# Three score chunks on each side of A@V: regrouping the bursts of a fused attention and feed-forward kernel

## The chip, the cores and the metric

The kernel runs on one core of a Trainium2 chip. The metric is the device time of one execution in microseconds (us); the time before is the median of five executions.

## The reference

For each of 8 batches and 12 heads, attention without a softmax over 448 positions of 64 features; then a feed-forward layer with a parametric ReLU over the 3584 x 768 result.

```python
scores = scale * np.matmul(q, k.transpose(0, 1, 3, 2))      # scale = 1/8
attn = np.maximum(scores, 0.0) ** 2 / S                     # S = 448
attn_out = np.matmul(attn, v)
x = attn_out.transpose(0, 2, 1, 3).reshape(B * S, H * D)    # 3584 x 768
h = x @ w_in                                                # 768 x 2048
g = np.maximum(h, 0.0) + alpha * np.minimum(h, 0.0)
out = g @ w_out                                             # 2048 x 768
```

## The kernel before, in words

**Units of work.** Four heads of one batch form a group; there are 24 groups, three to a batch. A group is cut into seven score *chunks*. `score_mm` (L171) does a chunk with four matmuls of 64x64 weights over 448 columns, which occupy the four quarters of the TensorE array together, so four of them take the place of one ("a wave"). A chunk fills two neighbouring PSUM banks. `relu` (L182) takes both banks to SBUF in one instruction, on ScalarE (line 185) for a chunk marked "A", on VectorE (line 187) for one marked "D". `square` (L190) squares it in SBUF, on VectorE (L195) or ScalarE (L193). `attnv` (L198) multiplies the seven squared chunks of a group by V: 28 matmuls in seven waves (L205) into a pair of banks, whose first bank ScalarE (L215) and whose second bank VectorE (L216) then scale into `xT`.

`f1` (L252) makes one of 16 blocks of the hidden layer of a batch: six 128x128 matmuls over 448 columns (L239), then ScalarE (L247) and VectorE (L248) evict it into `gT`. `f2` (L257) makes 128 rows by 384 columns of the output: 16 matmuls (L262), one copy out of PSUM (L264, on ScalarE), and two output DMAs from SyncE's queue (L270).

**PSUM.** There are eight banks, handed out in the program's order. `take_bank` gives the bank that was taken longest ago; `take_pair` gives the pair (0-1, 2-3, 4-5, 6-7) whose later-taken bank was taken longest ago:

```python
lo = min((0, 2, 4, 6), key=lambda i: (max(taken[i], taken[i + 1]), i))
i = min(range(8), key=lambda i: (taken[i], i))
```

The first matmul into a bank waits until the engine that evicts the bank's last content is done.

**Order.** It is written out by hand; every engine runs its instructions in the order of the program. `sc` (L220) does chunks up to the relu, `sq` (L225) the squares that are still due, `run` (L230) both. A *plain burst* is `run(some(3))`: three chunks between two `f1` or two `f2`. A *full burst* is `burst(n)` (L394): three chunks, `attnv(n)`, two chunks, all squares on VectorE. Chunks marked A, D, A in turn (`some`, L389).

Groups 0 to 5 and the first hidden layer are an opening written out line by line up to L383. From L386 on, chunks of groups 6 to 23 are taken from one list. During batch 1 (L401 to L438) there are four plain bursts and full bursts 6, 7 and 8. Then the loop over batches 2 to 7 (L440): 16 `f1`, with plain bursts ahead of blocks 6 and 12, then six or eight `f2` units with three full bursts, each behind an `f2`. The last batch has no bursts. In batch 6 the list runs out: its second full burst has only one chunk behind `attnv`, its third none.

**Loads.** `prepare(n)` (L343) readies group n: two copies on VectorE (L162), a DMA transpose into `T` from SyncE's queue (L164), and the loads of q, k and v of group n+2 from GpSimd's queue (L97, L104). `turn_pe` (L143) does the same with 28 transposes on TensorE and two copies.

Of the kernel before, what the change touches and what calls it, by code (L numbers as in the profile page):

```python
# [16 lines left out]
NJ = 7  # L17
# [3 lines left out]
def kernel(  # L21
# [10 lines left out]
    nc = tc.nc  # L32
    B, H, S, D = q.shape
# [6 lines left out]
    HALF = d_model // 2  # L40
# [43 lines left out]
    def take_bank():  # L84
        i = min(range(8), key=lambda i: (taken[i], i))
        take(i, 1)
        return psum[:, i]
# [4 lines left out]
    def load_qk(n):  # L92
        b, g = divmod(n, NG)
        for name, src in (("q", q), ("k", k)):
            t = raw_pool.tile([128, 2, NJ, D], BF16, tag=name, name=f"{name}raw")
            flat = src[b].rearrange("(m two) (pp j) d -> (two pp) m (j d)", two=2, j=NJ)
            nc.gpsimd.dma_start(out=t.rearrange("p m j d -> p m (j d)"), in_=flat[:, 2 * g:2 * g + 2])  # L97
            raw[(n, name)] = t
# [44 lines left out]
    def turn_pe(n, cuts=((0, NJ, "D"),), cuts_k=((0, NJ, "D"),)):  # L143
        t = T_pool.tile([128, 2, NJ, 128], BF16, tag="T", name="T")
        for i, name in enumerate("qk"):
            src = raw.pop((n, name))
            for lo, hi, eng in (cuts, cuts_k)[i]:
                ps = take_bank().bitcast(BF16)
                for j in range(lo, hi):
                    for s in range(2):  # L150
                        nc.tensor.transpose(ps[64 * s:64 * s + 64, 128 * j:128 * j + 128], src[:, s, j], ident)  # L151
                dst = t[:, i, lo:hi].rearrange("p j c -> p (j c)")
                if eng == "D":
                    nc.vector.tensor_copy(dst, ps[:, 128 * lo:128 * hi])  # L154
                else:
                    nc.scalar.copy(dst, ps[:, 128 * lo:128 * hi])
        T[n] = t

    def turn_dma(n):
        p = perm_pool.tile([128, 2, NJ, 2, D], BF16, tag="perm", name="perm")  # L160
        for i, name in enumerate("qk"):
            nc.vector.tensor_copy(p[:, i], raw.pop((n, name)).rearrange("p s j d -> p j s d"))  # L162
        t = T_pool.tile([128, 2, NJ, 128], BF16, tag="T", name="T")
        nc.sync.dma_start_transpose(out=t.rearrange("p a j c -> p (a j) c"),  # L164
                                    in_=p.rearrange("p a j s d -> p (a j s d)"))
        T[n] = t
# [4 lines left out]
    def score_mm(n, j):  # L171
        ps = take_pair()
        t = T[n]
        for r in range(2):
            for c in range(2):
                nc.tensor.matmul(ps[64 * c:64 * c + 64, r, :S],  # L176
                                 t[64 * r:64 * r + 64, 1, j, 64 * c:64 * c + 64],
                                 t[64 * r:64 * r + 64, 0, :, 64 * c:64 * c + 64],
                                 start=True, stop=True)
        return ps  # L180

    def relu(ps, eng):  # L182
        rl = rl_pool.tile([128, 2, S], BF16, tag="rl", name="rl")
        if eng == "A":
            nc.scalar.activation(rl, ps[:, :, :S], ACTF.Relu)  # L185
        else:
            nc.vector.tensor_scalar(rl, ps[:, :, :S], 0.0, None, ALU.max)  # L187
        return rl

    def square(n, j, rl, eng="D"):  # L190
        a = at_pool.tile([128, 2, S], BF16, tag="at", name="at")
        if eng == "A":
            nc.scalar.activation(a, rl, ACTF.Square)  # L193
        else:
            nc.vector.tensor_tensor(a, rl, rl, ALU.mult)  # L195
        att[(n, j)] = a

    def attnv(n):  # L198
        ps = take_pair()
        vv = vraw.pop(n)  # L200
        for j in range(NJ):
            a = att.pop((n, j))
            for r in range(2):
                for s in range(2):
                    nc.tensor.matmul(ps[64 * s:64 * s + 64, r, :S],  # L205
                                     vv[64 * r:64 * r + 64, s, j, :],
                                     a[64 * r:64 * r + 64, s],
                                     start=(j == 0), stop=(j == NJ - 1))
        b, g = divmod(n, NG)
        if g == 0:  # L210
            xT[b] = xT_pool.tile([128, NG, 2, S], BF16, tag="xT", name="xT")
        if n == 0:
            nc.scalar.activation(xT[b][:, g], ps[:, :, :S], ACTF.Copy, scale=out_scale)
            return
        nc.scalar.activation(xT[b][:, g, 0], ps[:, 0, :S], ACTF.Copy, scale=out_scale)  # L215
        nc.vector.tensor_scalar(xT[b][:, g, 1], ps[:, 1, :S], out_scale, None, ALU.mult)  # L216
# [3 lines left out]
    def sc(chunks):  # L220

        for n, j, eng in chunks:
            late.append((n, j, relu(score_mm(n, j), eng)))

    def sq(k=99, eng="D"):  # L225
        for g in late[:k]:
            square(*g, eng)
        del late[:k]

    def run(chunks):  # L230
        sc(chunks)
        sq()
# [21 lines left out]
        f1_mm(ps, b, ff, range(KM))  # L254
        f1_out(ps, b, ff)

    def f2(sb, c, hf, parts=((0, HALF),)):  # L257
        o = o_pool.tile([128, HALF], F32, tag="o", name="osb")
        for lo, hi in parts:
            ps = take_bank()[:, :hi - lo]  # L260
            for ff in range(KF):
                nc.tensor.matmul(ps, gT[sb][:, ff, bass.ts(c, 128)], w_out_sb[:, hf, ff, lo:hi],  # L262
                                 start=(ff == 0), stop=(ff == KF - 1))
            nc.scalar.copy(o[:, lo:hi], ps)  # L264
            for u in range(2):
                blk = 2 * c + u
                b, j = 2 * sb + blk // NJ, blk % NJ
                rows = out[b * S:(b + 1) * S].rearrange("(pp j) d -> j pp d", j=NJ)
                eng = nc.scalar if u and hi - lo < HALF else nc.sync
                eng.dma_start(out=rows[j][:, hf * HALF + lo:hf * HALF + hi], in_=o[64 * u:64 * u + 64, lo:hi])  # L270


    pat = "ADAAAAA"
# [1 line left out]
    def ch(n, lo, hi, p=pat):  # L275
        return [(n, j, p[j]) for j in range(lo, hi)]
# [57 lines left out]
    def f1s(b, lo, hi):  # L334
        for ff in range(lo, hi):
            f1(b, ff)

    def load(n):
        if n < NQ:
            load_qk(n)  # L340
            load_v(n)

    def prepare(n):  # L343
        if n < NQ:
            turn_dma(n)
        load(n + 2)
# [9 lines left out]
    ps = take_bank()[:, :S]  # L356
# [5 lines left out]
    f1s(0, 10, 12)  # L362
    sc(ch(3, 6, 7) + ch(4, 0, 2, "AA"))
    f1s(0, 12, 16)
    f2(0, 0, 0)
    sc(ch(4, 2, 5, "AAADAAA"))
    attnv(3)
    sc(ch(4, 5, 7, "AAAAAAD"))
    turn_pe(5)
    sq(3)  # L370
    sq(2, "A")
    load_qk(8)
    load_v(8)
    f2(0, 1, 0)
    sc(ch(5, 0, 3))
    attnv(4)
    sc(ch(5, 3, 5, "AAAADAA"))
    sq(3)
    sq(2, "A")
    f2(0, 2, 0)  # L380
    sc(ch(5, 5, 7, "AAAAAAD"))
    sq(1, "A")
    sq(1)  # L383


    chunks = [(n, j) for n in range(2 * NG, NQ) for j in range(NJ)]  # L386
# [2 lines left out]
    def some(k):  # L389
        lo = at_c[0]  # L390
        at_c[0] = min(lo + k, len(chunks))
        return [(n, j, e) for (n, j), e in zip(chunks[lo:at_c[0]], "ADA")]

    def burst(n):  # L394

        sc(some(3))
        attnv(n)
        sc(some(2))
        sq()

    early = []  # L401
    for ff in range(4):
        ps = take_bank()[:, :S]
        f1_mm(ps, 1, ff, range(4))
        early.append(ps)
        if ff == 1:
            attnv(5)
    for ff in range(KF):
        if ff < 4:
# [15 lines left out]
    f2(0, 1, 1)  # L425
    run(some(3))
    f2(0, 2, 1)
    run(some(3))
    f2(0, 4, 0)
    burst(6)  # L430
    f2(0, 4, 1)
    f2(0, 5, 0)
    prepare(10)
    burst(7)
    f2(0, 5, 1)
    f2(0, 6, 0)
    burst(8)
    f2(0, 6, 1)  # L438

    for b in range(2, B):  # L440
        n0 = NG * (b + 1)
        last = b == B - 1
        sb = b // 2
        for ff in range(KF):
            if not last and ff in (6, 12):
                run(some(3))
            if not last and ff in (1, 9):
                prepare(n0 + 2 + ff // 8)
            f1(b, ff)
        if b % 2 == 0:  # L450
            units = [(sb, c, h) for c in range(3) for h in range(2)]
            at = {1: 0, 3: 1, 5: 2}
        else:
            units = [(sb, c, h) for c in range(3, 7) for h in range(2)]
            at = {1: 0, 4: 1, 7: 2}
        for i, u in enumerate(units):
            if i in at and not last:
                g = at[i]
                if g == 1:
                    prepare(n0 + 4)  # L460
                burst(n0 + g)
            if last and i == len(units) - 1:
                f2(*u, parts=((0, 256), (256, HALF)))
            else:
                f2(*u)


# [28 lines left out]
```

## Time and profile before

| What | Value |
|---|---|
| Median of five executions | 389.18 us (389.0 to 389.33) |
| Profiled execution, its own time | 389.2 us |
| Its span, first to last instruction | 387.4 us |
| Around the span | 1.8 us |
| TensorE matmul (PE) busy | 378.4 us (98%) |
| VectorE (DVE) busy | 266.0 us (69%) |
| ScalarE (ACT) busy | 206.4 us (53%) |
| Granted TensorE clock, mean | 0.998 |

PE stands for TensorE's matmuls, PEld for its weight loads, DVE for VectorE, ACT for ScalarE, POOL for GpSimd, SP for SyncE. A row of the timeline gives the start, the length, the engine, the line, the operation and the tiles of an instruction, or of several alike that are merged (x12). The chain of work lists, in order of time, what the end of the execution goes back to. TensorE's matmuls overlap in the array, so a matmul is shown longer than the distance to the next one; in this text what counts for TensorE is the distance from start to start. A matmul's output in the tables is named `psum`, whatever its bank.

### The profile page before, as it was taken

The page shows a single profiled execution, that of the slowest core. Times are in us where ns is not written, and L with a number is a line of the kernel's source. Part 1 is how long each engine was busy: PE and PEld are TensorE (multiplying, and loading weights), DVE is VectorE, ACT ScalarE, POOL GpSimd, SP SyncE. Part 2 cuts the span into 40 slices and gives each one's busy share as a digit, 9 for nine tenths or more (in the row PEclk, how much of TensorE's full clock was granted, in tenths as well). Part 3 has the DMA queues.
Part 4 walks back from the last instruction along what each step waited for, and adds up shares of the span by engine and source line. Part 5 has one row for each costly group of instructions (what it writes and reads, how often), then busy time and mean ns, then how long its engine had stood idle before and what let it go on. Part 6 is the DMA issues. An engine that isn't in the chain of part 4 may idle for free.

```text
span 387.4 us, 7916 instructions
## 1 busy us (share of the span) xinstructions
PE 378.4 (98%) x3228; PEld 211.7 (55%) x3228; DVE 266.0 (69%) x420; ACT 206.4 (53%) x332; POOL 63.3 (16%) x94
## 2 busy tenths in 40 slices
PE   7799999999999999999999999999999999999995
PEld 6444564555665456645555455654555545655564
DVE  3977876777868878789655896689754887626300
ACT  4977686355555664455445554547543475434311
POOL 7566211512022202022110221120000000000000
PEclk9999999999999999999999999999999999999999
DMA  9999999999393775687192871937035300120023
GB/s 182 187 203 204 204 213 212 149 171 192 101 169 52 118 134 76 127 139 117 44 175 51 137 119 42 178 55 136 22 72 99 70 0 23 42 61 2 19 71 76
DMA packets 71093, 43.06 MB, mean 111 GB/s; under 512 B 38160, under 2 KB 71056, under 8 KB 71056
## 3 DMA queue, kind: packets, MB, share of 16 engines
q0 software_dynamic: 26496, 22.35, 39.5%
q1 hardware_dynamic: 44128, 19.65, 24.2%
q8 instruction: 25, 0.41, 0.5%
q10 hardware_dynamic: 432, 0.56, 0.4%
q14 instruction: 12, 0.10, 0.1%
HBM read 45.62 MB, written 11.01 MB: 146 GB/s over the span
## 4 chain that ended last, share of the span: by engine, by line
PE 94%; DVE 2%; ACT 1%; DMA 1%; issue 1%; ACTq 0%
PE psum L239 38%; PE psum L262 38%; PE psum L176 9%; PE psum L205 8%; ACT rl L185 1%; DMA qfirst<-in_q_dram 1%; PE psum L151 1%; DVE at L195 1%; DVE T L154 0%; DVE rl L187 0%; ACT osb L264 0%; ACTq L270 0%; DVE qraw L134 0%; ACT xT L215 0%; ACTq L264 0%
## 5 line engine op out<-in xcount | busy, mean ns | idle before, releaser
L262 PE MATMUL psum<-w_out_sb,gT 128*128 128x384 bf16 (+2 forms) x912 | 151.1, 323 | 0.0
L239 PE MATMUL psum<-xT,w_in_sb 128*128 128x448 bf16 x768 | 149.5, 353 | 0.4 <-ACT rl L185 0.4
L262 PEld LDWEIGHTS <-gT 128*128 128x128 bf16 x912 | 86.7, 98 | 63.0 <-issue 8.2
L239 PEld LDWEIGHTS <-w_in_sb 128*128 128x128 bf16 x768 | 73.7, 98 | 72.4 <-issue 6.0
L248 DVE SCALAR_TENSOR_TENSOR gT<-neg,beta_sb,psum 128x448 bf16<-128x448 f32 x128 | 83.2, 676 | 30.8 <-ACT neg L247 30.6
L247 ACT ACTIVATE neg<-psum 128x448 f32<-128x448 f32 x128 | 69.2, 546 | 64.1 <-PE psum L239 60.3
L185 ACT ACTIVATE rl<-psum 128x896 bf16<-128x896 f32 x112 | 97.4, 937 | 1.1 <-PE psum L176 1.1
L195 DVE TENSOR_TENSOR at<-rl 128x896 bf16<-128x896 bf16 x162 | 90.7, 616 | 0.0
L187 DVE TENSOR_SCALAR rl<-psum 128x896 bf16<-128x896 f32 x56 | 60.8, 1086 | 41.7 <-PE psum L176 41.5
L264 ACT COPY osb<-psum 128x384 f32<-128x384 f32 (+2 forms) x57 | 27.0, 473 | 105.6 <-PE psum L262 100.9
L176 PE MATMUL psum<-T 64*64 64x448 bf16 x672 | 45.7, 356 | 2.7 <-DVE T L154 0.9
L97 POOL DMA_DIRECT2D qraw<-in_q_dram x23 | 16.5, 719 | 171.8 <-DVE perm L162 166.9
L205 PE MATMUL psum<-at,vraw 64*64 64x448 bf16 x672 | 37.0, 351 | 0.5 <-ACT rl L185 0.2
L205 PEld LDWEIGHTS <-vraw 64*64 64x64 bf16 x672 | 24.2, 106 | 10.8 <-issue 2.9
L176 PEld LDWEIGHTS <-T 64*64 64x64 bf16 x672 | 18.1, 105 | 21.8 <-issue 15.1
L216 DVE TENSOR_SCALAR xT<-psum 128x448 bf16<-128x448 f32 x23 | 14.4, 624 | 16.2 <-PE psum L205 11.8
L97 POOL DMA_DIRECT2D kraw<-in_k_dram x23 | 16.6, 722 | 14.5 <-PE psum L239 7.5
L104 POOL DMA_DIRECT2D vraw<-in_v_dram x24 | 17.5, 731 | 1.4 <-DMA vraw<-in_v_dram 0.5
L215 ACT ACTIVATE xT<-psum 128x448 bf16<-128x448 f32 x23 | 12.7, 552 | 3.0 <-PE psum L205 3.0
L162 DVE COPY perm<-qraw 128x896 bf16<-128x896 bf16 x18 | 11.0, 611 | 3.5 <-DMA T<-perm 2.4
L114 POOL DMA_DIRECT2D w_in_sb<-in_moe_w_in_dram x16 | 10.1, 630 | 7.8 <-DMA w_in_sb<-in_moe_w_in_dram 3.0
L162 DVE COPY perm<-kraw 128x896 bf16<-128x896 bf16 x18 | 10.9, 607 | 0.0
(22 smaller groups left out, 41.9 us busy)
## 6 DMA issues: line engine op xcount, KB each, us to landing
out_dram<-osb SPq DMA_DIRECT2D x110, 96.0 KB, 2.2
vraw<-in_v_dram POOLq DMA_DIRECT2D x24, 224.0 KB, 7.4
qraw<-in_q_dram POOLq DMA_DIRECT2D x23, 224.0 KB, 4.7
kraw<-in_k_dram POOLq DMA_DIRECT2D x23, 224.0 KB, 6.6
w_in_sb<-in_moe_w_in_dram POOLq DMA_DIRECT2D x16, 192.0 KB, 8.4
w_out_sb<-in_moe_w_out_dram POOLq DMA_DIRECT2D x2, 1536.0 KB, 18.5
qfirst<-in_q_dram SPq DMA_DIRECT2D x1, 448.0 KB, 4.3
kfirst<-in_k_dram ACTq DMA_DIRECT2D x1, 448.0 KB, 4.6
```

Of the source, the lines that this page charges most:

```text
L97: nc.gpsimd.dma_start(out=t.rearrange("p m j d -> p m (j d)"), in_=flat[:, 2 * g:2 * g + 2])
L162: nc.vector.tensor_copy(p[:, i], raw.pop((n, name)).rearrange("p s j d -> p j s d"))
L176: nc.tensor.matmul(ps[64 * c:64 * c + 64, r, :S], t[64 * r:64 * r + 64, 1, j, 64 * c:64 * c + 64], t[64 * r:64 * r + 64, 0, :, 64 * c:64 * ...
L185: nc.scalar.activation(rl, ps[:, :, :S], ACTF.Relu)
L187: nc.vector.tensor_scalar(rl, ps[:, :, :S], 0.0, None, ALU.max)
L195: nc.vector.tensor_tensor(a, rl, rl, ALU.mult)
L205: nc.tensor.matmul(ps[64 * s:64 * s + 64, r, :S], vv[64 * r:64 * r + 64, s, j, :], a[64 * r:64 * r + 64, s], start=(j == 0), stop=(j == NJ ...
L239: nc.tensor.matmul(ps, w_in_sb[:, km // 2, km % 2, bass.ts(ff, 128)], xT[b][:, km // 2, km % 2, :], start=(km == 0), stop=(km == KM - 1))
L247: nc.scalar.activation(neg, ps, ACTF.Relu, scale=-1.0)
L248: nc.vector.scalar_tensor_tensor(gT[b // 2][:, ff, (b % 2) * S:(b % 2) * S + S], neg, beta_sb[:, ff:ff + 1], ps, ALU.mult, ALU.add)
L262: nc.tensor.matmul(ps, gT[sb][:, ff, bass.ts(c, 128)], w_out_sb[:, hf, ff, lo:hi], start=(ff == 0), stop=(ff == KF - 1))
L264: nc.scalar.copy(o[:, lo:hi], ps)
```

## The change

1. `burst(n)` takes three chunks behind `attnv` instead of two. Of its squares, five are on VectorE and the last on ScalarE.
2. Batches 2 to 6 have one plain burst in the `f1` blocks (ahead of block 6) instead of two. Batch 1 has three plain bursts instead of four.
3. `f2` can copy its output on VectorE. It does so for each `f2` directly ahead of a full burst (`eng="D"`), 20 of the 56 units.
4. `prepare` stands ahead of `f1` blocks 1, 8 and 13 instead of ahead of blocks 1 and 9 and the second full burst; in batch 1 `prepare(10)` stands ahead of one `f2` instead of behind it.
5. The opening: its last three bursts of 3+2, 3+2 and 2 chunks become two of 3+3; `turn_pe(5)` stands ahead of the first of them, with the q copy on ScalarE; `attnv(5)` stands behind three partial `f1` blocks instead of two.

All matmuls, relus, squares, copies and transfers stay the same in number and shape.

```diff
-    def f2(sb, c, hf, parts=((0, HALF),)):
+    def f2(sb, c, hf, parts=((0, HALF),), eng="A"):
...
-            nc.scalar.copy(o[:, lo:hi], ps)
+            (nc.vector.tensor_copy if eng == "D" else nc.scalar.copy)(o[:, lo:hi], ps)
...
-    f2(0, 0, 0)
+    f2(0, 0, 0, eng="D")
+    turn_pe(5, ((0, NJ, "A"),))
     sc(ch(4, 2, 5, "AAADAAA"))
     attnv(3)
-    sc(ch(4, 5, 7, "AAAAAAD"))
-    turn_pe(5)
+    sc(ch(4, 5, 7, "AAAAAAD") + ch(5, 0, 1))
     sq(3)
-    sq(2, "A")
+    sq(1, "A")
+    sq()
     load_qk(8)
     load_v(8)
     f2(0, 1, 0)
-    sc(ch(5, 0, 3))
+    f2(0, 2, 0, eng="D")
+    sc(ch(5, 1, 4, "AADAAAA"))
     attnv(4)
-    sc(ch(5, 3, 5, "AAAADAA"))
+    sc(ch(5, 4, 7, "AAAAADA"))
     sq(3)
-    sq(2, "A")
-    f2(0, 2, 0)
-    sc(ch(5, 5, 7, "AAAAAAD"))
     sq(1, "A")
     sq(1)
+    sq(1, "A")
...
         sc(some(3))
         attnv(n)
-        sc(some(2))
-        sq()
+        sc(some(3))
+        sq(5)
+        sq(1, "A")
...
-        if ff == 1:
+        if ff == 2:
             attnv(5)
...
     f2(0, 2, 1)
-    run(some(3))
-    f2(0, 4, 0)
+    f2(0, 4, 0, eng="D")
     burst(6)
     f2(0, 4, 1)
-    f2(0, 5, 0)
     prepare(10)
+    f2(0, 5, 0, eng="D")
     burst(7)
     f2(0, 5, 1)
-    f2(0, 6, 0)
+    f2(0, 6, 0, eng="D")
     burst(8)
...
-            if not last and ff in (6, 12):
+            if not last and ff == 6:
                 run(some(3))
-            if not last and ff in (1, 9):
-                prepare(n0 + 2 + ff // 8)
+            if not last and ff in (1, 8, 13):
+                prepare(n0 + 2 + (1, 8, 13).index(ff))
...
             if i in at and not last:
-                g = at[i]
-                if g == 1:
-                    prepare(n0 + 4)
-                burst(n0 + g)
+                burst(n0 + at[i])
...
-                f2(*u)
+                f2(*u, eng="D" if i + 1 in at and not last else "A")
```

More of the change, by code (lines that the diff above doesn't have):

```diff
@@ L268, in f2 @@
                 rows = out[b * S:(b + 1) * S].rearrange("(pp j) d -> j pp d", j=NJ)
-                eng = nc.scalar if u and hi - lo < HALF else nc.sync
-                eng.dma_start(out=rows[j][:, hf * HALF + lo:hf * HALF + hi], in_=o[64 * u:64 * u + 64, lo:hi])
+                queue = nc.scalar if u and hi - lo < HALF else nc.sync
+                queue.dma_start(out=rows[j][:, hf * HALF + lo:hf * HALF + hi], in_=o[64 * u:64 * u + 64, lo:hi])
     pat = "ADAAAAA"
```

## The prediction

> **What bounds the kernel.** I read the busy times first, then the chain of work, then the timeline of one batch, and last the single full burst, where the change acts.
>
> ```profile
> PE 378.4 (98%) x3228; PEld 211.7 (55%) x3228; DVE 266.0 (69%) x420; ACT 206.4 (53%) x332; POOL 63.3 (16%) x94
> PE 94%; DVE 2%; ACT 1%; DMA 1%; issue 1%; ACTq 0%
> ```
>
> TensorE is the bound almost throughout: 94% of the chain that ends last is its own, at a granted clock of 0.998. No engine's relief can help by itself; only what makes TensorE's instructions closer together or further apart counts. The chain in order of time shows what bursts cost (start, length, what, both in us):
>
> ```profile
> 163.04 6.81 PE psum L239 x36
> 169.85 0.69 PE psum L176 x12
> 170.54 6.92 PE psum L239 x36
> 177.46 0.69 PE psum L176 x12
> 178.15 4.65 PE psum L239 x24
> 182.79 2.60 PE psum L262 x16
> 185.39 0.69 PE psum L176 x12
> 186.09 1.39 PE psum L205 x28
> 187.48 0.38 PE psum L176 x8
> 187.86 7.91 PE psum L262 x48
> ```
>
> A wave of four 64x64 matmuls costs 0.38/2 = 0.19 once it follows others. But a plain burst of three waves costs 0.69, and the 36 matmuls behind it 6.92 instead of 6.81: 0.80 for what is worth 0.57. The other 0.23 is entering and leaving. The timeline of the full burst at 185.32 has the evictions:
>
> ```profile
> 185.32 0.76 PE L176 MATMUL psum<-T 64*64 64x448 bf16 x12
> 185.43 0.48 ACT L264 COPY osb<-psum 128x384 f32<-128x384 f32 x1 [2.06 <-PE psum L262]
> 185.81 1.73 ACT L185 ACTIVATE rl<-psum 128x896 bf16<-128x896 f32 x2
> 185.95 1.09 DVE L187 TENSOR_SCALAR rl<-psum 128x896 bf16<-128x896 f32 x1 [1.86 <-PE psum L176]
> 185.96 1.52 PE L205 MATMUL psum<-at,vraw 64*64 64x448 bf16 x28
> 187.28 0.58 PE L176 MATMUL psum<-T 64*64 64x448 bf16 x8
> 187.51 0.54 ACT L215 ACTIVATE xT<-psum 128x448 bf16<-128x448 f32 x1
> 187.55 0.62 DVE L216 TENSOR_SCALAR xT<-psum 128x448 bf16<-128x448 f32 x1 [0.51 <-PE psum L205]
> ```
>
> Two things are to be seen. A@V starts 0.05 after the copy of the last `f2` ends (185.43 + 0.48 = 185.91): following `take_pair` by hand, A@V's pair holds that `f2`'s bank. And the following `f2` starts at 187.79, 2.47 after the burst's start, while the eviction of A@V by ScalarE runs until 188.05; today that harms nothing, since this `f2` takes a bank of the burst's third chunk.
>
> **Removed: entries and exits.** Batch 1 and batches 2 to 6 lose one plain burst each: 6 x 0.80 = -4.80. The opening's last burst of two chunks goes: its 0.50 on the chain and 0.11 behind it, -0.61. The waves do not go; they return below.
>
> **Full bursts: the third chunk behind A@V.** 17 bursts are concerned (three in batch 1, three in each of batches 2 to 5, two in batch 6). It adds a wave (0.19; in the last of the 17, two), and with it a change of banks. Three chunks, A@V and three chunks take all eight banks, so the next `f2` gets the oldest, the first bank of A@V's own pair. Its first matmul must now wait for ScalarE's L215, and everything on TensorE is queued behind that matmul.
>
> **Full bursts: the copy on VectorE.** No row has VectorE copying 128x384 fp32 out of PSUM. From L187 and L216 (896 columns 1.086, 448 columns 0.624): 1.03 ns a column and 0.162 fixed, so 0.56. From below, the cast of 512 fp32 columns that VectorE reads from SBUF took 0.427, scaled 0.36; from above, L248's 0.676 for 448, scaled 0.60. I take 0.56: L187 and L216 read fp32 from PSUM as this copy does. The copy starts 0.04 later than on ScalarE (L216 starts 0.04 after L215), so at 0.15 from the burst's start; it ends at 0.71 and A@V may write its bank at 0.76 instead of 0.64: +0.12.
>
> The Trainium skill (VectorE: DVE Perf Modes, section "Why PSUM operands drop a tier") speaks against this move: a PSUM operand has one read port for VectorE, so fp32 gets one element a cycle. The errata table of that page gives 120 + 384 cycles, an estimate of 0.53 by its 0.96 GHz; for L216's 448 columns it gives 0.59 where the trace has 0.624. By the page the sum would be 17 x 0.03 = 0.5 lower than mine.
>
> Together, from the burst's start: L215 starts at 2.19 + 0.12 = 2.31, ends at 2.85 (0.54), and `f2` starts at 2.85 + 0.05 = 2.90. Without the bank's wait it would be 2.47 + 0.12 + 0.19 = 2.78. So the wait is 0.12. Its bounds: 0, if another bank is taken or if leaving the 64x64 mode takes as long anyway; 0.22, if L215 starts 0.10 late.
>
> Before, these 17 bursts took to their next block 7.42 in batch 1 (2.50, 2.46, 2.46), 7.38 in batches 2 and 4 (2.46 on average), 7.45 in 3 and 5 (2.47, 2.47, 2.51), and 2.47 and 2.27 in batch 6: 41.82. After: 17 x 2.90 = 49.30. That is +7.48: 18 waves of 0.19 (3.42), 17 later copies (about 2.0) and 17 bank waits (about 2.0).
>
> **The opening.** Burst 3 has `turn_pe(5)`'s 0.90 between `f2` and itself, which covers the copy: A@V starts 0.05 earlier than now, `f2` is released at 2.14 + 0.54 + 0.05 = 2.73: +0.26. Burst 4 goes to 2.90: +0.43. With -0.61, +0.08. `attnv(5)` meets its last square about when it needs it (three partial blocks, 12 x 0.19 = 2.3, and six waves lie ahead of it); I put that at 0, at most 0.3.
>
> **What costs nothing, and its cover.** ScalarE gets a relu and a square (0.98) more behind a burst: xT to 2.85, two relus to 4.5, the square to 5.4; the next `f2` copy is wanted at 2.90 + 2.60 + 0.1 = 5.6. VectorE ends its five squares at about 6.6 (now 6.5); the next copy ahead of a burst is wanted at 8.2 or later. If that 1.5 were gone, the copy and with it A@V would be late by the rest. `prepare` moves past `f1` work: two VectorE copies of 0.61, one transpose DMA on SyncE's queue (7.0 to landing, its group is first read a batch stage later), three loads on GpSimd's queue (4.7 to 7.4; the copies that need them come 14 us later). Behind block 13 the two copies put `gT` of block 15 back by some 0.5 after catching up; the first `f2` needs it 15 x 0.16 = 2.4 after its start. In the `f2` stage SyncE's output DMAs lose a transpose ahead of them, which today takes 2.47 of that queue.
>
> **The sum.** -4.80 + 7.48 + 0.08 = +2.76 on the span, 390.2. The profiled execution took 389.2 for a span of 387.4, and the median of the runs is 389.18, so both starting points agree: 392.0.
>
> **Rivals.** Forecast (0.66): both waits stand; with the copy's and the wait's bounds 391.2 to 393.5.
>
> *The copy is short* (0.12; the rival on the other side). If VectorE copies in 0.42 or less, it ends before 0.59, where A@V starts without any wait (the burst at 150.04 starts it at 150.63). Then the bank is free at 2.73: 17 x 2.73 = 46.41, +4.59 - 4.80 - 0.09 = -0.3: 388.9, no change. For it: the 0.427 of the cast. Against: that one reads SBUF.
>
> *Neither wait* (0.09). In addition the bank costs nothing, `f2` starting at 2.47 - 0.05 + 0.19 = 2.61: 44.37, +2.55 - 4.80 - 0.33 = -2.6: 386.6. For it: fewer entries is what remains. Against: bank order is fixed by the program.
>
> *Only the copy's wait* (0.06): 2.78 each, 47.26, +5.44 - 4.80 - 0.16 = +0.5: 389.7.
>
> *VectorE late* (0.07): if the copy ahead of a burst queues behind squares or `prepare`, by 0.2 each time 3.4 more, 395.4. Against: the margin of 1.5 above.
>
> **Numbers.** Differences below 0.2% (0.8 us) can hardly be measured here. Faster takes the third case and a part of the second (0.13), the same most of the second and the fourth (0.14), slower the rest (0.73). The range, 388.0 to 394.0, holds the forecast, the short copy and the copy alone; it leaves out the third case and the far part of the fifth.
>
> **What would show it.** In the profile after, from a full burst's start: the VectorE copy at 0.15, 0.56 long; A@V's second pair of matmuls at 0.76; L215 at 2.31; `f2` at 2.90 and named as waiting for xT L215; 0.80 less for each plain burst gone. A copy of 0.4 or `f2` at 2.6 would make me wrong, as would a TensorE wait inside the `f1` stage.

## The result and the profile after

| | Before | After |
|---|---|---|
| Median | 389.18 us | 389.96 us |
| Ratio to before, 95% interval | | 1.0021 [1.0015, 1.0027] |
| Profiled execution, its own span | 387.4 us | 388.0 us |
| VectorE busy | 266.0 us | 262.5 us |
| ScalarE busy | 206.4 us | 219.9 us |

The change makes the kernel slower by 0.8 us, a fifth of a per cent; that is small, but the whole interval lies above 1. The forecast was 392.0, 2.8 above the kernel before: the side was right, the size three and a half times too large. The page's row of the copies on VectorE:

```profile
L264 DVE COPY osb<-psum 128x384 f32<-128x384 f32 x20 | 11.2, 558 | 40.4 <-PE psum L262 40.4
```

A copy takes 558 ns on average, as estimated. In the chain of work in order of time (start, length, what), the plain bursts cost and save what was predicted, but the full bursts are of two kinds. Here is a full burst of batch 2 and then a stretch of batch 3 up to its first full burst:

```profile
149.56 0.69 PE psum L176 x12
150.26 1.47 PE psum L205 x28
151.72 0.57 PE psum L176 x12
152.29 5.31 PE psum L262 x32
...
163.03 6.81 PE psum L239 x36
169.84 0.69 PE psum L176 x12
170.53 11.46 PE psum L239 x60
181.99 2.60 PE psum L262 x16
184.59 0.69 PE psum L176 x12
185.28 1.53 PE psum L205 x28
186.81 0.53 ACT xT L215
187.34 0.04 issue
187.38 7.96 PE psum L262 x48
```

The `f1` stage takes 6.81 + 0.69 + 11.46 = 18.96 instead of 19.76: the 0.80 of one plain burst. In the burst at 184.52 the chain leaves TensorE for 0.53 of ScalarE's L215: the bank's wait, now on the chain that sets the end of the execution. In the burst at 149.50 it never leaves TensorE. The timelines of the two bursts tell why. First the burst of batch 3:

```profile
184.52 0.76 PE L176 MATMUL psum<-T 64*64 64x448 bf16 x12
184.63 0.56 DVE L264 COPY osb<-psum 128x384 f32<-128x384 f32 x1 [1.34 <-PE psum L262]
184.93 0.11 PEld L205 LDWEIGHTS <-vraw 64*64 64x64 bf16 x1
...
185.24 1.52 PE L205 MATMUL psum<-at,vraw 64*64 64x448 bf16 x28
...
186.79 0.54 ACT L215 ACTIVATE xT<-psum 128x448 bf16<-128x448 f32 x1
...
187.38 0.32 PE L262 MATMUL psum<-w_out_sb,gT 128*128 128x384 bf16 x1
```

and the second burst of batch 2:

```profile
149.50 0.76 PE L176 MATMUL psum<-T 64*64 64x448 bf16 x12
149.60 0.56 DVE L264 COPY osb<-psum 128x384 f32<-128x384 f32 x1 [1.66 <-PE psum L262]
149.90 0.11 PEld L205 LDWEIGHTS <-vraw 64*64 64x64 bf16 x3
...
150.09 1.64 PE L205 MATMUL psum<-at,vraw 64*64 64x448 bf16 x28
...
151.62 0.54 ACT L215 ACTIVATE xT<-psum 128x448 bf16<-128x448 f32 x1
...
152.23 0.50 PE L262 MATMUL psum<-w_out_sb,gT 128*128 128x384 bf16 x2
```

In the first, one weight load goes ahead and A@V's first matmul waits until the copy is done: A@V starts at 0.72 from the burst's start, L215 at 2.27, `f2` at 2.86. In the second, three weight loads go ahead: the first two matmuls, into the pair's first bank, start at 0.59, and only the third, into the second bank, waits until 0.72. The first bank's sums end earlier, L215 starts at 2.12, and `f2` at 2.73. Of the 17 bursts nine are of the first kind and eight of the second. Following `take_bank` and `take_pair` through the whole program gives the same nine and eight: in the nine the last `f2`'s bank is the first (even) one of the pair that A@V takes, in the eight it is the second (odd) one.

The parts add up. Full bursts: 9 x 2.86 + 8 x 2.73 = 47.58 against 41.82, +5.76. Plain bursts: -4.80. The opening, from the first chunks of group 3 to the `f2` ahead of the first plain burst: 80.36 - 31.30 = 49.06 against 80.46 - 31.54 = 48.92, +0.14. A sum of +1.1; the chains from those chunks of group 3 to the end of the last `f2` on the chain differ by (383.46 - 31.30) - (382.68 - 31.54) = 352.16 - 351.14 = +1.02.

### The profile page after: what moved, and what is told of

Same layout as the page of the kernel before. It is cut to its first block, busy times and chain, and to the rows that moved or that the text cites. A ratio compares the mean times of both kernels' runs of the same rounds, so it can differ in the third digit from the quotient of the medians.

```text
span 388.0 us, 7937 instructions
## 1 busy us (share of the span) xinstructions
PE 378.2 (97%) x3228; PEld 214.2 (55%) x3228; DVE 262.5 (68%) x418; ACT 219.9 (57%) x334; POOL 63.3 (16%) x94
## 4 chain that ended last, share of the span: by engine, by line
PE 93%; ACT 2%; DVE 2%; DMA 1%; issue 0%; ACTq 0%
PE psum L262 38%; PE psum L239 38%; PE psum L205 9%; PE psum L176 7%; ACT xT L215 1%; DMA qfirst<-in_q_dram 1%; DVE at L195 1%; PE psum L151 1%; DVE T L154 1%; ACT rl L185 1%; DVE rl L187 1%; ACT kraw L134 0%; ACT osb L264 0%; ACTq L270 0%; ACT qraw L134 0%
## 5 line engine op out<-in xcount | busy, mean ns | idle before, releaser
L262 PE MATMUL psum<-w_out_sb,gT 128*128 128x384 bf16 (+2 forms) x912 | 150.6, 323 | 0.5
L185 ACT ACTIVATE rl<-psum 128x896 bf16<-128x896 f32 x118 | 101.3, 932 | 44.6 <-PE psum L176 44.6
L262 PEld LDWEIGHTS <-gT 128*128 128x128 bf16 x912 | 87.5, 98 | 63.1 <-issue 7.9
L195 DVE TENSOR_TENSOR at<-rl 128x896 bf16<-128x896 bf16 x147 | 82.1, 616 | 0.0
L187 DVE TENSOR_SCALAR rl<-psum 128x896 bf16<-128x896 f32 x50 | 54.3, 1086 | 3.3 <-PE psum L176 3.2
L176 PE MATMUL psum<-T 64*64 64x448 bf16 x672 | 45.5, 355 | 2.3 <-ACT rl L185 0.8
L264 ACT COPY osb<-psum 128x384 f32<-128x384 f32 (+2 forms) x37 | 17.4, 472 | 40.3 <-PE psum L262 39.0
L264 DVE COPY osb<-psum 128x384 f32<-128x384 f32 x20 | 11.2, 558 | 40.4 <-PE psum L262 40.4
L205 PE MATMUL psum<-at,vraw 64*64 64x448 bf16 x672 | 37.8, 351 | 0.5 <-ACT rl L185 0.2
L176 PEld LDWEIGHTS <-T 64*64 64x64 bf16 x672 | 20.6, 106 | 19.1 <-issue 12.4
L205 PEld LDWEIGHTS <-vraw 64*64 64x64 bf16 x672 | 24.5, 106 | 11.8 <-issue 5.7
L216 DVE TENSOR_SCALAR xT<-psum 128x448 bf16<-128x448 f32 x23 | 14.4, 625 | 13.0 <-PE psum L205 13.0
L193 ACT ACTIVATE at<-rl 128x896 bf16<-128x896 bf16 x21 | 20.1, 963 | 0.5
L215 ACT ACTIVATE xT<-psum 128x448 bf16<-128x448 f32 x23 | 12.7, 552 | 6.1 <-PE psum L205 5.0
```

Of the source, the lines that this page charges most:

```text
L176: nc.tensor.matmul(ps[64 * c:64 * c + 64, r, :S], t[64 * r:64 * r + 64, 1, j, 64 * c:64 * c + 64], t[64 * r:64 * r + 64, 0, :, 64 * c:64 * ...
L205: nc.tensor.matmul(ps[64 * s:64 * s + 64, r, :S], vv[64 * r:64 * r + 64, s, j, :], a[64 * r:64 * r + 64, s], start=(j == 0), stop=(j == NJ ...
L264: (nc.vector.tensor_copy if eng == "D" else nc.scalar.copy)(o[:, lo:hi], ps)
```

## The experiments

The theory after the traces: the copy on VectorE holds up A@V in all 17 bursts; the bank's wait comes on top in the nine where A@V's first half is held up. The rivals were that ScalarE needed the relief, that leaving the 64x64 mode costs as much as the bank's wait, and that the two kinds of burst differ by their place.

**1. All copies on ScalarE (`e1_copy_act`)**

```diff
-            (nc.vector.tensor_copy if eng == "D" else nc.scalar.copy)(o[:, lo:hi], ps)
+            nc.scalar.copy(o[:, lo:hi], ps)
```

> The changed kernel with every f2 copy back on ScalarE; the bursts stay 3+3. Theory (the copy's end holds up A@V, and through L215 the next f2): the copy ends at 0.59 from the burst's start instead of 0.67; in the 9 of 17 bursts where its bank is the first of A@V's pair, f2 comes at 2.78 instead of 2.86, in the other 8 at 2.72 instead of 2.73. That is 0.8 less: 389.1. Rival (ScalarE needs the relief, since its relus now start 0.05 to 0.1 later and L215 behind them): f2 later than 2.86, time above 390.2.

Measured 388.97, ratio to before 0.999 [0.9976, 1.0003]. The bursts of the first kind reach `f2` at 2.78, of the second at 2.72, as expected (one of the second at 2.75, where the copy started 0.04 late). So the copy on VectorE costs the change 1.0 us by the medians, some 0.8 by the bursts' starts; with ScalarE it would be level with the kernel before. ScalarE needed no relief.

**2. No wait for A@V's bank (`e2_shared_pair`)**

```diff
-    def score_mm(n, j):
-        ps = take_pair()
+    def score_mm(n, j, ps=None):
+        if ps is None:
+            ps = take_pair()
...
-        sc(some(3))
+        behind = some(3)
+        sc(behind[:1])
+        if len(behind) == 3:
+            (n4, j4, e4), (n5, j5, e5) = behind[1:]
+            ps = score_mm(n4, j4)
+            rl = relu(score_mm(n5, j5, ps), e5)
+            late.append((n4, j4, rl))
+            late.append((n5, j5, rl))
```

> The changed kernel, but in each of the 17 bursts the fifth and the sixth chunk write the same pair of banks, one after the other, and one relu takes them out (left out: the fifth chunk's scores, whose place the sixth's take, and one relu on VectorE). TensorE's work is the same; the next f2 finds a bank that was free at 2.2, so it waits for nothing behind A@V. Theory (f2 waits for L215 in the 9 bursts where the copy's bank is the first of the pair): these go from 2.86 to 2.74, the other 8 stay at 2.73: 1.1 less, 388.9. Rival (leaving the 64x64 mode costs as much as the wait): no change, 390.0. The prediction on record (17 waits of 0.12): 2.0 less, 388.0.

Measured 388.76, 0.9989 [0.9973, 1.0004]. `f2` comes at 2.74 in the nine bursts (in the one below, 187.24 - 184.50; this kernel's L177, L206, L216 and L263 are L176, L205, L215 and L262 of the others) and stays at 2.73 in the eight.

```profile
184.50 0.76 PE L177 MATMUL psum<-T 64*64 64x448 bf16 x12
185.22 1.52 PE L206 MATMUL psum<-at,vraw 64*64 64x448 bf16 x28
186.54 0.76 PE L177 MATMUL psum<-T 64*64 64x448 bf16 x12
...
186.77 0.55 ACT L216 ACTIVATE xT<-psum 128x448 bf16<-128x448 f32 x1
...
187.24 0.34 PE L263 MATMUL psum<-w_out_sb,gT 128*128 128x384 bf16 x1
```

The eviction of A@V still runs until 187.32 here, and TensorE no longer minds. The wait is real, it is the bank's, and leaving the 64x64 mode does not hide it. It was worth 0.12 in nine bursts, not in 17: in the other eight the copy sets the pace. There the bank's wait lies close below: with the copy taken away (run 1) they only go to 2.72, 0.05 behind the end of L215.

**3. Neither wait (`e3_shared_pair_copy_act`)**: the edits of 1 and 2 together.

> Both of the last two edits together: copies on ScalarE and the shared pair (left out as there). Theory: with neither wait TensorE goes through the burst at its own pace, f2 at 2.66 in all 17 bursts: 17 x 2.66 against 47.6 measured, 2.4 less, 387.5; that is what fewer bursts alone would be worth, 1.7 below the kernel before. Rival (a third limit behind both, such as ScalarE's relus or the change of modes): not below 388.7.

Measured 387.44, 0.9952 [0.9933, 0.997]: 1.7 below before, with `f2` at 2.65 or 2.66 in 16 of the 17. This is where the gain of fewer bursts goes: 2.5 us lie between this run and the change, and they are the two waits: by the bursts' starts 9 x (2.86 - 2.66) + 8 x (2.73 - 2.65) = 2.4. No third limit showed itself down to there; 2.65 is the 2.46 of the kernel before and one wave of 0.19.

**4. The older bank first (`e4_older_bank_first`)**

```diff
+    def take_split():
+        lo = min((0, 2, 4, 6), key=lambda i: (max(taken[i], taken[i + 1]), i))
+        old, new = (lo, lo + 1) if taken[lo] <= taken[lo + 1] else (lo + 1, lo)
+        take(lo, 2)
+        taken[new] += 0.5
+        return old, new
...
-                    nc.tensor.matmul(ps[64 * s:64 * s + 64, r, :S],
+                    dst = psum[64 * s:64 * s + 64, banks[r], :S] if n else ps0[64 * s:64 * s + 64, r, :S]
+                    nc.tensor.matmul(dst,
```

`banks = take_split()` stands for the pair (group 0 keeps `take_pair`), and the lines that were L215 and L216 evict `banks[0]` and `banks[1]`; the next `f2` gets `banks[0]`.

> The changed kernel with one edit: A@V's first half goes into that bank of its pair that was taken longer ago, and the next f2 takes that bank; the copy on VectorE stays. So the copy's bank is always the one that A@V's second half writes. Theory (the step of the prediction that failed is which bank the copy holds): the 9 bursts at 2.86 go to 2.73, the 8 others stay: 1.2 less, 388.8. Rival (the two groups of bursts differ by where they stand, after f1 or between f2, and not by the bank): no change, 390.0.

Measured 388.85, 0.9991 [0.9975, 1.0007]. All 17 bursts now reach `f2` at 2.73. The burst that was at 2.86 in batch 3 starts A@V at 185.00 - 184.41 = 0.59 (its L183, L215 and L272 are `score_mm`, A@V and `f2`):

```profile
184.41 0.76 PE L183 MATMUL psum<-T 64*64 64x448 bf16 x12
185.00 1.64 PE L215 MATMUL psum<-at,vraw 64*64 64x448 bf16 x28
...
187.14 0.34 PE L272 MATMUL psum<-w_out_sb,gT 128*128 128x384 bf16 x1
```

So it is the bank that makes the two kinds, not their place.

**5. The older bank first, copies on ScalarE (`e5_older_first_copy_act`)**: the edits of 1 and 4 together.

> The older bank first in A@V and all copies on ScalarE, on the changed kernel: the version that the runs so far point to. Theory: the copy never holds up A@V's first half, L215 starts at 2.12 behind ScalarE's second relu, and f2 comes at 2.12 + 0.54 + 0.05 = 2.72 in all 17 bursts: 1.4 below the changed kernel, 388.6, some 0.6 below the kernel before. Rival (ScalarE's copy pushes its relus and L215 back where the copy's bank no longer matters): not below 388.9.

Measured 388.36, 0.9979 [0.997, 0.9988]. `f2` comes at 2.72 in 16 of the 17. This version leaves nothing out and beats both kernels: by 0.8 us the one before, by 1.6 the changed one. What is left to run 3 is that `f2` still waits for L215, whose 0.54 the three waves do not quite cover.

**6. The copies alone on the kernel before (`e6_before_copy_dve`)**

```diff
-                f2(*u)
+                f2(*u, eng="D" if i + 1 in at and not last else "A")
```

and the same for the three `f2` ahead of bursts 6, 7 and 8.

> The kernel before with one part of the change alone: the f2 copy ahead of each of the 18 full bursts 6 to 23 on VectorE; the bursts stay 3+2 and two plain bursts a batch. Theory: the copy ends at 0.67 from the burst's start instead of 0.59, A@V's waiting matmuls start at 0.72 instead of 0.64; nothing else is waited for, so all of it reaches the next f2: about 0.08 in 14 bursts, 0.04 in the three whose copy started late anyway, 1.2 in all: 390.4. Rival (the move to VectorE gains by freeing ScalarE for the relus): 389.2 or less.

Measured 393.32 (four executions, 392.75 to 393.85), 1.011 [1.0095, 1.0126]: both theories missed it. Most bursts behave as the theory had it, with `f2` at 2.54 or 2.55. But in five middle bursts it comes at 3.08. VectorE's rows of one of them:

```profile
150.97 0.56 DVE L264 COPY osb<-psum 128x384 f32<-128x384 f32 x1 [1.36 <-PE psum L262]
...
151.44 0.61 DVE L162 COPY perm<-qraw 128x896 bf16<-128x896 bf16 x1
...
151.97 0.61 DVE L162 COPY perm<-kraw 128x896 bf16<-128x896 bf16 x1
...
152.49 1.08 DVE L187 TENSOR_SCALAR rl<-psum 128x896 bf16<-128x896 f32 x1
...
153.63 0.38 PE L176 MATMUL psum<-T 64*64 64x448 bf16 x4 [0.35 <-DVE rl L187]
```

In the kernel before, `prepare` stands between that `f2` and the burst. With the copy on ScalarE, VectorE does the two perm copies while `f2` still runs (in the trace of before at 148.71 and 149.24, ahead of the burst at 150.04). With the copy on VectorE, they queue behind a copy that waits for that `f2`, and the relu of the second chunk queues behind them: it ends 1.0 later (2.71 from the burst's start, against 1.71 in the burst at 149.50 of the changed kernel), and the chunk that needs its banks is late.

**7. The same with prepare moved as in the change (`e7_before_copy_dve_prepare`)**

```diff
-            if not last and ff in (1, 9):
-                prepare(n0 + 2 + ff // 8)
+            if not last and ff in (1, 8, 13):
+                prepare(n0 + 2 + (1, 8, 13).index(ff))
...
-                if g == 1:
-                    prepare(n0 + 4)
```

> The last run (kernel before, copies ahead of the 18 full bursts on VectorE) with prepare moved as in the change: ahead of blocks 1, 8 and 13, and in batch 1 ahead of the f2. Theory from that run's trace (in its six middle bursts two perm copies of 0.61 lie behind the copy and ahead of the relu on VectorE, and the next f2 comes at 3.08 instead of 2.54): the middle bursts fall back to 2.54 and only the copy's own 0.08 each stays: 390.4. Rival (the copy itself makes VectorE's relus late, wherever prepare stands): above 391.5.

(It was five middle bursts, not six: in batch 6 `prepare` has nothing left to do.) Measured 390.23, 1.0025 [1.0016, 1.0035]. The middle bursts are at 2.54 or 2.55, and what stays is the copy's own delay, 0.08 in most bursts. So the move of `prepare` is what makes the copy on VectorE affordable: 3.1 us by the medians, 5 x 0.54 = 2.7 by the bursts' starts.

**8. The move of prepare alone (`e8_before_prepare`)**

> The kernel before with the move of prepare alone (copies on ScalarE, 3+2 bursts, two plain bursts). Theory: its copies on VectorE and its transfers lie beside other work in both places: 389.2, no change. Rival (two copies behind block 13 put gT of block 15 back beyond the 2.4 that the first f2 leaves): each of five batches later by up to 0.5, above 390.

Measured 389.25, 1.0 [0.9991, 1.0009]: no change. With the copy on ScalarE it does not matter where `prepare` stands.

## Why the prediction was right or wrong

**Right, to a hundredth or two.** 0.80 for each plain burst, seen six times. A wave of 0.19 for the added chunk. The copy's 0.56, taken by the rows that read fp32 from PSUM; the Trainium skill (VectorE: DVE Perf Modes, "Why PSUM operands drop a tier" and the errata table) gives one read port as the reason, which no run here tests, and, at an estimated 0.53, a slightly short time; the trace's 0.558 decides. That A@V would wait for that copy, and that `f2` would wait for L215: runs 1 and 2 take each of them away. That ScalarE and VectorE have room behind a burst: the copy starts at 0.11 in all 17. That `prepare` costs nothing in its new place: run 8 and the absence of TensorE waits in the `f1` stage.

**Wrong: one step.** "L215 starts at 2.19 + 0.12 = 2.31" was applied to all 17 bursts. It holds only where the copy's bank is the first of A@V's pair. The prediction followed `take_pair` far enough to see that the pair holds the last `f2`'s bank, and did not ask which of the two it is. In eight bursts it is the second; L215 starts at 2.12 and `f2` at 2.73 instead of 2.90: 8 x 0.17 = 1.4 too much. Run 4 shows it by making it the second in all bursts. The trace of before already had the two kinds. In its bursts at 99.18 (second kind) and 206.06 (first kind) the copy on ScalarE starts equally late, at 0.15; in the one A@V starts ahead of the copy's end, in the other 0.05 behind it:

```profile
99.33 0.48 ACT L264 COPY osb<-psum 128x384 f32<-128x384 f32 x1 [1.29 <-issue]
...
99.78 1.60 PE L205 MATMUL psum<-at,vraw 64*64 64x448 bf16 x28
...
206.21 0.48 ACT L264 COPY osb<-psum 128x384 f32<-128x384 f32 x1 [2.12 <-PE psum L262]
...
206.74 1.52 PE L205 MATMUL psum<-at,vraw 64*64 64x448 bf16 x28
```

The prediction read one burst of the first kind, the one at 185.32, and took it for all: its 2.19 for L215 holds in seven of the 17 bursts of before; in two more of the first kind, whose copy started late, it is 2.23, and in the eight of the second kind 2.12 or 2.13. The "17 later copies (about 2.0) and 17 bank waits (about 2.0)" came to 5.76 - 3.42 = 2.3 together. That the measured 389.96 lies next to the 389.7 of the rival "only the copy's wait" is chance: the eight bursts come near what that rival describes (2.78 each), in the other nine both waits stand.

**A term mis-sized.** The copy was put at 0.15 from the burst's start, by L216's start behind L215's. It starts at 0.11, as ScalarE's did, so the nine bursts are at 2.86 and not at 2.90: 9 x 0.04 = 0.4. Together these are 1.7, as much as lies between the predicted +2.76 and the chain's +1.02. The profiled spans differ by less than the chain, 388.0 - 387.4 = 0.6: the trace of after is 0.24 ahead when the chunks at 31.30 begin (31.54 before), and between the last matmuls on the chain and ScalarE's copy it has 0.04 of "issue" where before has 0.33. Why these two parts differ stays open, as does the rest of the way to the medians' 0.78.

**The opening: right by luck.** +0.08 was predicted and +0.14 seen, but its two bursts are off by 0.20 and 0.17, in opposite directions. Burst 4 is of the second kind and reaches `f2` at 2.73 instead of 2.90. Burst 3 reaches it at 52.42 - 49.49 = 2.93 instead of 2.73:

```profile
49.21 0.91 ACT L156 COPY T<-psum 128x896 bf16<-128x896 bf16 x1 [2.57 <-PE psum L151]
...
49.49 1.05 PE L176 MATMUL psum<-T 64*64 64x448 bf16 x12
49.60 0.62 DVE L154 COPY T<-psum 128x896 bf16<-128x896 bf16 x1 [0.35 <-PE psum L151]
...
50.28 1.59 PE L205 MATMUL psum<-at,vraw 64*64 64x448 bf16 x28
```

`turn_pe(5)` does cover the copy of `f2`, as predicted, but its transposes take two banks of their own. By `take_pair` the third chunk's pair holds the bank that ScalarE empties until 50.12, and A@V's first bank is the one that VectorE empties until 50.22. So A@V starts at 0.79 from the burst's start and not, as predicted, at 0.59. No run changes this alone; in run 4, where A@V's first half takes the other bank of that pair, it starts at 0.69.

**A cover that was named too lightly.** The prediction gave the queue ahead of the copy (VectorE late by squares or `prepare`) and found a margin of 1.5. It did not ask about the queue behind the copy, where the margin is much smaller: in run 6 two perm copies there make a relu 1.0 late, and that costs 0.54 a burst.

## What to carry to other kernels

When a bank, buffer or pair is handed out by age, follow the allocation to the single bank and to the engine that empties it: here the even or odd bank decided 0.13 us a burst; choosing it on purpose took 1.1 us off the changed kernel (run 4), and with the copies back on ScalarE the loss of 0.8 became a gain of 0.8 (run 5). When a group of work grows until it takes every buffer, what follows it waits for an eviction of that same group, so price the saved switches against that wait. A copy that is moved to another engine takes its wait with it: what stands behind it in that engine's order is late too (run 6).

## What the runs showed of the hardware that was not expected

The four quarters of a 64x64 wave need not go together. Where only the matmuls into the second bank wait, the first two start on their own: in the burst at 149.50 A@V takes 1.64 from first start to last end instead of the 1.52 of the burst at 184.52, its two halves 0.13 apart, and the half that was not held up ends 0.15 earlier, which is why its eviction can start earlier. The Trainium skill (TensorEngine Tiling (Array Packing), section "Key Properties") says that tiles run independently; this is that independence in a number, at a lag that is shorter than one wave of 0.19. No run here shows a longer lag.
